# Depthwise convolutions of the gate on VectorE instead of TensorE, with dP copies moved to ScalarE and half of the X sums to GpSimd

## The chip, the cores and the metric

The kernel runs on one core of one Trainium2 chip. The metric is the device time of one execution in microseconds (us). TensorE is written PE, VectorE DVE, ScalarE ACT, GpSimd POOL and SyncE SP, as in the profile; PEld is the weight loading of PE.

## The reference

Forward and backward pass of a speech block with an attention branch and a gated convolution branch, for x of 2 x 4000 x 144 (batch, tokens T, channels D) in bfloat16. The outputs are the block's output and the gradients of x and of seven weights. Cut to what matters here:

```python
def _fwd_reference(x, w_qkv, w_att_out, w_mlp_in, dw_csgu, w_mlp_out, dw_merge, w_merge):
    xa = _layernorm(x)
    q, k, v = split(xa @ w_qkv)
    p = softmax(q @ k^T * D ** -0.5)             # 4000 x 4000 for each batch
    glob = (p @ v) @ w_att_out
    u, g = split(gelu(_layernorm(x) @ w_mlp_in))
    g = _layernorm(g)
    gc[t] = sum over i in 0..4 of g[t + i - 2] * dw_csgu[i]     # depthwise, 5 taps
    loc = (u * gc) @ w_mlp_out
    m = concat(glob, loc);  mc = depthwise 5 taps of m with dw_merge
    return x + (m + mc) @ w_merge
_out, _vjp = jax.vjp(_fwd_reference, ...);  _grads = _vjp(grad_out)
```

The backward pass of the gate needs the same five-tap convolution a second time, with the taps reversed, from the gradient of `gc` to the gradient of the normalized `g`.

## The kernel before

A sequence of 4000 tokens is laid out as 125 partitions x 32 blocks: partition p holds the tokens 32p to 32p+31, so a block is one token of each partition. Shifting by a token is shifting by a block, except at the ends of a partition, where two blocks of halo are fetched from the neighbouring partition by a DMA.

`phase_att` does one batch. Its loop runs over t = 0 to 32, one block of query rows for each t, and a step of it holds:

- four *quads* (`quad`, tags q0 to q3): scores S of block t against 1000 keys, and dP of block t-1 against another 1000, into two PSUM tiles `ps` (a pool of two). PE writes each quad with four matmuls of 500 columns over 128 channels (L1130) and four over the remaining 16 (L1136).
- `S_min` (L1154): DVE negates S from PSUM into `Pbuf` in bfloat16 with a running minimum; `P_exp` (L1162) takes the exponential on ACT.
- `PdP`: dP times P into `Sbuf`. For three of the four quads ACT copies dP out of PSUM (L1175) and DVE multiplies in SBUF (L1177); for the fourth (`direct`, q == 3) DVE multiplies straight from PSUM (L1172).
- SP transposes P and P*dP by DMA (`PT`, `ST`), and PE forms Y (L1186) and Z (L1225) from them, 32 matmuls each.
- six *X groups* (`X_group`, tags x0 to x5; five of three blocks, the last of one): PE sums the gradient's contributions for key blocks (L1270), and DVE adds the PSUM result to the accumulator `acc` (L1276).
- a share of the *local units* of the gate branch (`local_units`). These go in 16 rounds for each batch, two blocks at a time: `z_unit`, `e_tanh`, `e_h`, `e_stats`, `dug_unit`, `e_gn`, `e_dgc`, `e_m`, `e_gp` for a new pair, and for an older pair `gc_unit`, `e_du`, `dgn_unit`, `e_dh`, `dhT_unit`, and every second round the weight gradients `dwc_unit` and `dwi_unit`.

The convolutions run on PE. `t_unit` transposes a pair's normalized gate and its gradient (L534), and a stack of five blocks of the 16 channels above 128 (L539); ACT copies the result to `gT` and `gS` (L540, L542). `gc_unit` (12 matmuls, L551 and L553) multiplies by diagonal matrices of the taps, and ACT copies its result to `gc` (L554). `dgn_unit` (12 matmuls, L566 and L568) does the gradient's convolution the same way, with one column more that yields its sum over the channels; DVE reads it from PSUM (L572, L576, L584). Small PSUM results, X groups among them, share the pool `ps_w`. The diagonal matrices are built in the head, by POOL (`conv` in `Head`, L291 to L305).

The order of each engine's instructions in the loop is not the program's. `Planner.plan` runs a list scheduler over all instructions of t = 2 to 30 (batch 0) and t = 0 to 30 (batch 1), with a cost for each instruction (`cost`) and a lead for each class of instruction (the table `LEAD`, added to its position in the program), and pins the order that it finds on PE, DVE, ACT, POOL and SP. The instructions of one engine then run strictly in that order.

Of the kernel before, what the change touches and what calls it, by code (L numbers as in the profile page):

```python
# [14 lines left out]
D = 144  # L15
DR = 16
# [92 lines left out]
class Head:  # L109
# [159 lines left out]
    def conv(self):  # L269
# [18 lines left out]
        colS = wt.tile([80, 2], BF, name="colS")  # L288
        with nc.allow_non_contiguous_dma(reason="tiny conv weight column"):
            for kk in range(5):  # L290
                nc.gpsimd.dma_start(colS[kk * DR:(kk + 1) * DR, 0:1], k.dw_csgu[kk:kk + 1, 128:D].rearrange("k c -> c k"))  # L291
                nc.gpsimd.dma_start(colS[(4 - kk) * DR:(5 - kk) * DR, 1:2], k.dw_csgu[kk:kk + 1, 128:D].rearrange("k c -> c k"))
        colS32 = wt.tile([80, 2], F32, name="colS32")
        nc.gpsimd.tensor_copy(colS32[:], colS[:])
        W.dgf = wp.tile([128, 5, 128], BF, name="dgf")
        W.dgm = wp.tile([128, 5, 144], BF, name="dgm")
        for kk in range(5):
            nc.gpsimd.tensor_scalar(W.dgm[:, kk, 1:129], ident[:], cols[:, 4, kk:kk + 1], 1.0, op0=ALU.mult, op1=ALU.mult)
        nc.gpsimd.tensor_copy(W.dgf[:], W.dgm[:, :, 1:129])
        nc.gpsimd.tensor_copy(W.dgm[:, :, 0:1], cols[:, 4, :].rearrange("p (a b) -> p a b", b=1))  # L300
        W.dgs = wp.tile([80, 2, 160], BF, name="dgs")
        nc.gpsimd.memset(W.dgs[:], 0.0)
        for s in range(2):
            nc.gpsimd.tensor_scalar(W.dgs[:, s, 128 + s:D + s], W.mask[:], colS32[:, s:s + 1], 1.0, op0=ALU.mult, op1=ALU.mult)
        nc.gpsimd.tensor_copy(W.dgs[:, 1, 0:1], colS32[:, 1:2])  # L305
# [114 lines left out]
XW = 160  # L420


def local_units(k, W, b, S, A, es, DHT, ps_w):
# [7 lines left out]
    gdr = [pl.tile([PB, 2, G2, D], BF, name="gd%d" % i) for i in range(NR + 3)]  # L431
    rem = pl.tile([PB, 2, NB + 4, DR], BF, name="gd_rem")

    def gd(c):
        return gdr[{0: NR, NG2: NR + 1, NG2 + 1: NR + 2}.get(c, c % NR)]
# [3 lines left out]
    gT = [pl.tile([128, 4, PB], BF, name="gT%d" % i) for i in range(4)]  # L439
    gS = [pl.tile([80, 4, PB], BF, name="gS%d" % i) for i in range(2)]  # L440
# [12 lines left out]
    gc = pl.tile([PB, G2, D], BF, name="l_gc")  # L453
    dd = pl.tile([PB, G2, 2 * D], BF, name="l_dd")
# [55 lines left out]
    def e_dgc(g):  # L510
        t = gd(g + 1)
        nc.vector.tensor_tensor(t[:, 1], dugr[slot(g)][:], hg[:, :, 0:D], op=ALU.mult)
        nc.gpsimd.tensor_copy(rem[:, :, G2 + G2 * g:2 * G2 + G2 * g, :], t[:, :, :, 128:D])
        if g == NG2 - 1:
            nc.sync.dma_start(gd(0)[1:PB], t[0:PB - 1])
            nc.gpsimd.tensor_copy(rem[:, :, 0:G2, :], gd(0)[:, :, :, 128:D])
        if g == 0:
            nc.sync.dma_start(gd(NG2 + 1)[0:PB - 1], t[1:PB])
            nc.gpsimd.tensor_copy(rem[:, :, NB + 2:NB + 4, :], gd(NG2 + 1)[:, :, :, 128:D])
# [9 lines left out]
    def t_unit(c, g):  # L529
        pt = ps_w.tile([128, 8, 128], BF, tag="w")  # L530
        t = gd(c)
        for a in range(2):
            for bi in range(G2):
                nc.tensor.transpose(pt[:, 2 * a + bi, 0:PB], t[:, a, bi, 0:128], W.ident[0:PB, 0:PB])  # L534
        if g is not None:
            for a in range(2):
                for bi in range(G2):
                    j = G2 * g + bi
                    nc.tensor.transpose(pt[0:80, 4 + 2 * a + bi, 0:PB], rem[:, a, j:j + 5, :].rearrange("p a b -> p (a b)"), W.ident[0:PB, 0:PB])  # L539
        nc.scalar.copy(gT[c % 4][:], pt[:, 0:4, 0:PB])  # L540
        if g is not None:
            nc.scalar.copy(gS[g % 2][:], pt[0:80, 4:8, 0:PB])  # L542

    def col(a, h):
        return gT[(h // G2) % 4][:, 2 * a + h % G2, :]

    def gc_unit(g):
        pc = ps_w.tile([PB, G2, D], F32, tag="w")
        for bi in range(G2):
            i = G2 * g + bi  # L550
            nc.tensor.matmul(pc[:, bi, :], gS[g % 2][:, bi, :], W.dgs[:, 0, 0:D], start=True, stop=False)  # L551
            for kk in range(5):
                nc.tensor.matmul(pc[:, bi, 0:128], col(0, i + kk), W.dgf[:, kk, :], start=False, stop=(kk == 4))  # L553
        nc.scalar.copy(gc[:], pc[:])  # L554
        ug = ugr[g % 2]
        nc.vector.tensor_tensor(ug[:], ur[slot(g)][:], gc[:], op=ALU.mult)
        nc.sync.dma_start(S.ug_d[:, G2 * g:G2 * g + G2, :], ug[:])
# [4 lines left out]
    def dgn_unit(g):  # L562
        pd = ps_w.tile([PB, G2, D + 1], F32, tag="w")
        for bi in range(G2):
            i = G2 * g + bi
            nc.tensor.matmul(pd[:, bi, :], gS[g % 2][:, 2 + bi, :], W.dgs[:, 1, 0:D + 1], start=True, stop=False)  # L566
            for kk in range(5):
                nc.tensor.matmul(pd[:, bi, 0:129], col(1, i + 4 - kk), W.dgm[:, kk, 0:129], start=False, stop=(kk == 4))  # L568
        rs, t = rsr[slot(g)], gd(g + 1)
        s2 = sm.tile([PB, G2], F32, tag="s2")  # L570
        for bi in range(G2):
            nc.vector.scalar_tensor_tensor(gc[:, bi, :], pd[:, bi, 1:D + 1], -1.0 / D, t[:, 0, bi, :], op0=ALU.mult, op1=ALU.mult, accum_out=s2[:, bi:bi + 1])  # L572
# [3 lines left out]
        nc.vector.scalar_tensor_tensor(c0[:], pd[:, :, 0], -1.0 / D, rs[:, 0:G2], op0=ALU.mult, op1=ALU.mult)  # L576
        for bi in range(G2):
            nc.gpsimd.tensor_scalar(w_[:, bi, :], t[:, 0, bi, :], nc1[:, bi:bi + 1], c0[:, bi:bi + 1], op0=ALU.mult, op1=ALU.add)
        live["pd"] = pd

    def e_dh(g):
        pd, rs = live["pd"], rsr[slot(g)]
        for bi in range(G2):
            nc.vector.scalar_tensor_tensor(dd[:, bi, D:2 * D], pd[:, bi, 1:D + 1], rs[:, bi:bi + 1], w_[:, bi, :], op0=ALU.mult, op1=ALU.add)  # L584
        nc.vector.tensor_tensor(dhr[g % 2][0:PB, :, 0:2 * D], dd[:], gpr[slot(g)][:], op=ALU.mult)
# [18 lines left out]
    def dwc_unit(g, part):  # L604
        pw = ps_w.tile([128, 512], F32, tag="w")
        bl = blocks(g)
        for n_, (gg, bi) in enumerate(bl):
# [6 lines left out]
            else:  # L614
                nc.tensor.matmul(pw[:, 0:128], gnb(i + 4), t[:, 1, bi, 0:128], start=first, stop=last, skip_group_check=True)
                nc.tensor.matmul(pw[0:80, 128:128 + D], rem[:, 0, i:i + 5, :].rearrange("p a b -> p (a b)"), t[:, 1, bi, :], start=False, stop=last, skip_group_check=True)
# [23 lines left out]
    def round_(n, o, c):  # L640
# [6 lines left out]
        tr = [(t_unit, c, c - 2 if c is not None and c >= 2 else None)]  # L647
# [4 lines left out]
        if c is None:  # L652
            tr = [None]
        for u_ in (new[0:3] + old[0:1] + new[3:5] + old[1:2] + new[5:7] + old[2:3] + new[7:9] + old[3:4] + new[9:10] + tr + end):
            if u_ is not None:
                add(*u_)
    round_(NG2 - 1, None, None)
    round_(0, None, 0)
    round_(1, None, 1)
    add(t_unit, 2, 0)  # L660
    for r in range(1, NG2 - 1):
        round_(r + 1 if r + 1 < NG2 - 1 else None, r - 1, r + 2)
    round_(None, NG2 - 2, NG2 + 1)
    round_(None, NG2 - 1, None)
# [5 lines left out]
dgn_un D.c:-370 D.l_gc:1726 D.nc:1278 P:-1400 P.l_w:2039  # L670
dhT_un S.dhT:-339
dug_un A.dugr:-1281 P:769
dwc_un0 A.l_fl:-1231 P:-2308 P.A_dwc:-176
dwc_un1 A.l_fl:-4398 P:-1151 P.A_dwc:-3945
dwi_un A.l_fl:-1330 P:204 P.A_dWiT:-1509
e_dgc D.gd:-543 P.gd_rem:-1405 S.gd:363
e_dh D.dhr:961 D.l_dd:235
e_du D.l_dd:2463
e_gn D.rsr:-997 P.gd:92
e_gp D.gpr:587 D.l_sq:1333  # L680
e_h D.l_hg:3382 P.l_q:2377
e_m D.l_z:1356 P.l_th:178
e_stat D.mv:-666 D.st:929 D.ve:1242 P.rsr:-5337 P.ur:-1767
e_tanh A.l_th:245 D.l_z:3163 P.l_a:-417
ex0 A.Pbuf:-3070
ex1 A.Pbuf:151
ex2 A.Pbuf:-598
ex3 A.Pbuf:1201
gc_uni A.l_gc:-3041 D.ugr:1422 P:-4451 S.ug_d:-2908
jm A.qz:2610 P:1843 P.qz:2359  # L690
jt S.qt:-2111
pd0 A.Sbuf:-3029 D.Sbuf:678
pd1 A.Sbuf:-34 D.Sbuf:-1662
pd2 D.Sbuf:1485
pd3 A.Sbuf:-3176 D.Sbuf:1319
pt S.PT:-1721
q0 P:800
q1 P:-1073
q2 P:-555
q3 P:-1767  # L700
sm0 D.Pbuf:-873
sm1 D.Pbuf:-191
sm2 D.Pbuf:-3971
sm3 D.Pbuf:-1539 D.nm:860
st0 S.ST:-357
st1 S.ST:-548
t_unit A.gS:1141 A.gT:-4603 P:-694
x0 D.acc:-903 P:-2106
x1 D.acc:-793 P:-110
x2 D.acc:-2067 P:1051  # L710
x3 D.acc:1510 P:725
x4 D.acc:-1103 P:-719
x5 D.acc:1346 P:2323
y0 P:1135
y1 A.ty:-43 A.yn:-422 D.dj:-4076 D.nd:-2446 D.rl:-1315 P:-1860 P.QBs:-1255 P.g:-2227 S.Yn_d:-1439
z0 P:1770
z1 D.qz:-99 P:756 S.Zn_d:-1843
z_unit0 A.l_hs:2644 A.l_sq:-515 P:-810
z_unit1 A.l_hs:1237 A.l_sq:1980 P:-1529 P.l_a:413
zt S.zt:1300  # L720
# [5 lines left out]
class Planner:  # L726
# [55 lines left out]
    def cost(self, e, ins):  # L782
# [14 lines left out]
        if e == "DVE":  # L797
# [10 lines left out]
            return d, d + 0.085  # L808
        if e == "Activation":
            d = (0.125 if n < 200 else 0.0) + (0.06 if psum else 0.05) + n * (0.00096 if kind == "InstActivation" and (n > 300 or not psum) else 0.00081)  # L810
# [4 lines left out]
        return d, d + 0.06  # L815
# [1250 lines left out]
```

## Time and profile before

| | |
|---|---|
| median of 3 runs | 1343.8 us (1340.99 to 1346.27) |
| the profiled execution | 1346.5 us, its span 1344.5 us, granted PE clock 0.966 |
| busy, us | PE 1269.1, PEld 1043.6, DVE 1055.5, ACT 762.5, POOL 545.8 |
| planned loops | from about 76 to 579 us and from about 705 to 1229 us of the span |
| DMA | 186.6 MB, mean 139 GB/s |

The remaining time is the head (weights, layer norm, the first two steps), the end of each batch (weight gradients, output) and the end of the kernel. Busy times of an engine are those in which at least one of its instructions runs; the time of a group of instructions in the profile is the sum over them, and neighbours can overlap by some tens of nanoseconds. The step from the start of one instruction to the start of the next one that follows at once is called its pitch here.

### The profile page before, as it was taken

What the parts mean: (1) busy time and instruction counts of PE and PEld (TensorE: products, weight loads), DVE (VectorE), ACT (ScalarE), POOL (GpSimd) and SP (SyncE); (2) the same over time, 40 slices, a digit from 0 to 9 for tenths busy, and PEclk for the clock granted to TensorE, in tenths of its full rate; (3) what the DMA queues carried; (4) which work ended last, traced back from release to release, by engine and by line L of the source; (5) the groups of instructions that cost most, each with busy time, mean ns of one, the idle gap of its engine ahead of it and who ended that gap; (6) DMA issues with size and microseconds to landing.
All of it is one profiled execution on the core that took longest, in us unless ns stands there. A gap on an engine that the chain in (4) does not pass through costs nothing.

```text
span 1344.5 us, 38722 instructions
## 1 busy us (share of the span) xinstructions
PE 1269.1 (94%) x15698; PEld 1043.6 (78%) x15698; DVE 1055.5 (79%) x2816; ACT 762.5 (57%) x1232; POOL 545.8 (41%) x1083
## 2 busy tenths in 40 slices
PE   5889999999999999978788999999999999999898
PEld 3557788788888777868785788788888887888897
DVE  7368989898888888856736897988888888887574
ACT  4656665666566665533625666566666566555381
POOL 7264344434334343237613443443434334334330
PEclk9799999999999999998897999999999999999899
DMA  4278998998989989965224999998988999988412
GB/s 120 53 135 135 165 149 147 160 156 148 157 150 150 153 143 160 144 142 160 66 66 83 168 161 154 154 151 144 160 160 144 163 155 156 158 164 172 131 43 72
DMA packets 629153, 186.64 MB, mean 139 GB/s; under 512 B 611951, under 2 KB 623873, under 8 KB 628932
## 3 DMA queue, kind: packets, MB, share of 16 engines
q1 hardware_dynamic: 623338, 171.84, 72.3%
q0 software_dynamic: 5088, 12.11, 3.4%
q8 instruction: 123, 2.02, 0.6%
q14 instruction: 56, 0.46, 0.1%
q10 hardware_dynamic: 548, 0.21, 0.1%
HBM read 21.04 MB, written 14.12 MB: 26 GB/s over the span
## 4 chain that ended last, share of the span: by engine, by line
PE 74%; DVE 10%; DMA 7%; ACT 3%; POOL 3%; issue 2%; SPq 0%; DVEq 0%; POOLq 0%; ACTq 0%
PE X L1270 18%; PE ps L1130 14%; PE yz L1225 9%; PE yz L1186 8%; PE ps L1136 6%; DMA ST<-Sbuf 3%; PE po L1619 3%; DVE Pbuf L1154 2%; PE pc L553 1%; DMA go_h<-in_grad_out_dram 1%; PE pj L1093 1%; PE pd L568 1%; DVE t L1645 1%; PE pd L501 1%; DVE acc L1276 1%
## 5 line engine op out<-in xcount | busy, mean ns | idle before, releaser
L1154 DVE TENSOR_SCALAR_CACHE_REDUCE Pbuf<-ps 125x1000 bf16<-125x1000 f32 x256 | 306.3, 1196 | 88.8 <-PE ps L1136 86.9
L1162 ACT ACTIVATE Pbuf<-Pbuf,nm 125x1000 bf16<-125x1000 bf16 x256 | 278.4, 1128 | 107.9 <-DVE nm L1156 107.5
L1270 PE MATMUL X<-QBs,Sbuf 125*125 125x144 bf16 x2048 | 301.9, 231 | 0.3 <-DVE acc L1276 0.3
L1270 PE MATMUL X<-QBs,Pbuf 125*125 125x144 bf16 x2048 | 296.7, 228 | 2.3 <-POOL QBs L1208 2.3
L1270 PEld LDWEIGHTS <-Sbuf 125*125 125x125 bf16 x2048 | 263.9, 139 | 29.2 <-issue 28.9
L1130 PE MATMUL ps<-xaT_m,qt 128*125 128x500 bf16 x1024 | 269.7, 383 | 8.8 <-DVE Pbuf L1154 2.9
L1175 ACT CAST Sbuf<-ps 125x1000 bf16<-125x1000 f32 x189 | 188.1, 995 | 142.9 <-PE ps L1136 141.9
L1270 PEld LDWEIGHTS <-Pbuf 125*125 125x125 bf16 x2048 | 265.1, 139 | 1.1 <-issue 1.0
L1276 DVE TENSOR_TENSOR acc<-X,acc 125x432 f32<-125x432 f32 x372 | 200.5, 550 | 48.4 <-PE X L1270 47.2
L1130 PEld LDWEIGHTS <-qt 128*125 128x125 bf16 x1024 | 124.7, 139 | 52.5 <-issue 9.6
L1225 PE MATMUL yz<-xa_aug,ST 125*125 125x144 bf16 x2048 | 155.0, 231 | 10.5 <-DMA ST<-Sbuf 8.3
L1225 PEld LDWEIGHTS <-ST 125*125 125x125 bf16 x2048 | 141.6, 140 | 21.6 <-DMA ST<-Sbuf 11.8
L1177 DVE TENSOR_TENSOR Sbuf<-Sbuf,Pbuf 125x1024 bf16<-125x1024 bf16 x189 | 135.1, 715 | 12.3 <-ACT Sbuf L1175 10.1
L1186 PE MATMUL yz<-xa_aug,PT 125*125 125x145 bf16 x2048 | 142.8, 228 | 1.1 <-DMA PT<-Pbuf 1.1
L1186 PEld LDWEIGHTS <-PT 125*125 125x125 bf16 x2048 | 136.1, 138 | 2.7 <-issue 1.3
L1136 PEld LDWEIGHTS <-qt 16*125 16x125 bf16 x1024 | 37.3, 129 | 103.7 <-issue 103.7
L1136 PE MATMUL ps<-XR,qt 16*125 16x500 bf16 x1016 | 114.2, 426 | 0.0
L1172 DVE TENSOR_TENSOR Sbuf<-ps,Pbuf 125x1000 bf16<-125x1000 f32 x67 | 79.9, 1192 | 3.7 <-PE ps L1136 2.3
L1105 POOL COPY qz<-qz 125x48 bf16<-125x48 bf16 x124 | 31.6, 284 | 109.0 <-ACT qz L1095 108.7
L1204 POOL TENSOR_SCALAR QBs<-qz,rl 125x144 bf16<-125x144 bf16 x64 | 25.1, 392 | 119.9 <-DVE rl L1192 90.2
L596 POOL TENSOR_TENSOR A_dwc<-l_fl,A_dwc 128x512 f32<-128x512 f32 (+2 forms) x48 | 37.5, 780 | 82.7 <-ACT l_fl L595 82.6
L1619 PE MATMUL po<-VUl,YT 128*125 128x144 bf16 x640 | 54.2, 232 | 7.1 <-ACT goT L352 7.1
(549 smaller groups left out, 2346.2 us busy)
## 6 DMA issues: line engine op xcount, KB each, us to landing
Yn_d<-yn SPq DMA_DIRECT2D x64, 35.2 KB
Zn_d<-qz SPq DMA_DIRECT2D x64, 35.2 KB
ug_d<-ugr SPq DMA_DIRECT2D x32, 70.3 KB
xo<-in_x_dram SPq DMA_DIRECT2D x16, 140.6 KB
out_dram<-dxo SPq DMA_DIRECT2D x16, 140.6 KB
go_h<-in_grad_out_dram POOLq DMA_DIRECT2D x4, 504.0 KB, 6.7
Zn<-Zn_d SPq DMA_DIRECT2D x4, 504.0 KB
ST<-Sbuf SPq DMA_TRANSPOSE x124
```

What stands on the lines that cost most here:

```text
L1130: mm = nc.tensor.matmul(pp[r // 2][:, r % 2, 0:CH], QT[i][:, 3 * h, 0:PB], xaTm[:, c * CH:(c + 1) * CH], start=True, stop=False)
L1136: nc.tensor.matmul(pp[r // 2][:, r % 2, 0:CH], QT[i][rs, 1 + h, 0:PB], xr, start=False, stop=True)
L1154: nc.vector.tensor_scalar(pv(Pbuf, i % NPB, c2), src, -1.0, 3.0e38, op0=ALU.mult, op1=ALU.min, accum_out=NM[i][:, c2:c2 + 1])
L1162: nc.scalar.activation(v, v, ACT.Exp, bias=NM[i][:, 4:5], scale=-1.0)
L1172: nc.vector.tensor_tensor(pv(Sbuf, i % NDB, c2), src, pv(Pbuf, i % NPB, c2), op=ALU.mult)
L1175: nc.scalar.copy(pv(Sbuf, i % NDB, c2), src)
L1177: nc.vector.tensor_tensor(sc, sc, pchunk(i % NPB, c2), op=ALU.mult)
L1186: nc.tensor.matmul(Y, PT[0:PB, j, 0:PB], xaa[:, j, 0:D + 1], start=(j == 0), stop=(j == NB - 1))
L1225: nc.tensor.matmul(Z, ST[0:PB, j, 0:PB], xaa[:, j, 0:D], start=(j == 0), stop=(j == NB - 1))
L1270: nc.tensor.matmul(X[:, jj, :], l, r, start=(n_ == 0), stop=(n_ == len(ops) - 1))
L1276: nc.vector.tensor_tensor(av, X[:, 0:nj, :], av, op=ALU.add)
L1619: nc.tensor.matmul(po[:, q, :], YT[h][:, (i + kk) * PB:(i + kk + 1) * PB], VU[h][:, kk, :], start=(n_ == 0), stop=False)
```

## The change

- `t_unit` is gone, with `gT`, `gS` and the diagonal matrices. The taps are kept as `W.cw`, one copy for each partition, loaded by one broadcast DMA, with a second, reversed set that POOL copies.
- `conv` on DVE: products of shifted blocks with the taps in bfloat16, SBUF to SBUF, then three additions. All blocks of the gate lie in one tile `gd`; a ring of five pairs plus three fixed ones breaks the run of shifts into pieces, one to seven products for each convolution. `gc_unit` and `dgn_unit` call it.
- the sum of the gradient over the channels (before, the extra PE column) is taken by ACT with an accumulating copy (`l_aj`).
- dP is copied by ACT in all four quads inside the loop (`DIRECT` is empty).
- X groups 0, 2 and 4 (`XP`), in the planned part of the loop: ACT copies PSUM to `xs` (two buffers, float32) and POOL adds to `acc`.
- `LEAD` has new values (before, from -5337 to 3382; now from -14396 to 11658), and some costs in `cost` are changed.

In numbers of instructions, over both batches: 272 transposes and 768 matmuls leave PE, with 68 PSUM copies of `t_unit` and 32 of `gc` on ACT. DVE gets 172 products (72 of 144 elements, 40 of 288, 28 of 864, 32 of 1440) and 192 additions (64 of 576, 128 of 288); 61 products from PSUM become products in SBUF; 162 additions to `acc` of 432 elements leave it. ACT gets 61 dP copies, 162 copies of X and 64 sums. POOL gets the 162 additions.

```diff
-        W.dgf, W.dgm, W.dgs = ...  (diagonal matrices; 10 small DMAs for their weights)
+        W.cw = wp.tile([PB, 2, 5, D], BF, name="cw")
+        nc.gpsimd.dma_start(W.cw[:, 0]..., k.dw_csgu...partition_broadcast(PB))
         for kk in range(5):
+            nc.gpsimd.tensor_copy(W.cw[:, 1, kk, :], W.cw[:, 0, 4 - kk, :])
...
-    def t_unit(c, g):
...
+    def conv(a, g, dst):
+        kk = 0
+        while kk < 5:
+            h = G2 * g + kk
+            q = pos(h)
+            n = 0
+            while kk + n < 5 and pos(h + n) == q + n and pos(h + n + 1) == q + n + 1:
+                n += 1
+            for bi in ((None,) if n else (0, 1)):
+                if bi is None:
+                    v = gdr[:, a, q:q + n + 1, :]
+                    v = bass.AP(v.tensor, v.offset, [list(v.ap[0]), [D, n], [D, G2], [1, D]])
+                    nc.vector.tensor_tensor(pr[:, kk:kk + n], v, W.cw[:, a, kk:kk + n, :]...to_broadcast([PB, n, G2, D]), op=ALU.mult)
+                else:
+                    nc.vector.tensor_tensor(pr[:, kk, bi, :], gdr[:, a, pos(h + bi), :], W.cw[:, a, kk, :], op=ALU.mult)
+            kk += max(n, 1)
+        nc.vector.tensor_tensor(pr[:, 0:2], pr[:, 0:2], pr[:, 2:4], op=ALU.add)
+        nc.vector.tensor_tensor(pr[:, 0], pr[:, 0], pr[:, 1], op=ALU.add)
+        nc.vector.tensor_tensor(dst[:], pr[:, 0], pr[:, 4], op=ALU.add)

     def gc_unit(g):
-        pc = ps_w.tile(...); 12 matmuls; nc.scalar.copy(gc[:], pc[:])
+        conv(0, g, gc)
...
     def dgn_unit(g):
-        pd = ps_w.tile(...); 12 matmuls
+        conv(1, g, dg)
+        s1 = sm.tile([PB, G2], F32, tag="s1")
         for bi in range(G2):
+            nc.scalar.activation(aj[:], dg[:, bi, :], ACT.Copy, accum_out=s1[:, bi:bi + 1])
...
-                    PdP(t - 1, q ^ 1, ps[1], q == 3)
+                    PdP(t - 1, q ^ 1, ps[1], q in DIRECT)
...
+            elif blocks[0] // 6 in XP and u0 <= here["t"] < NB - 1:
+                xs = XS[0].tile([PB, 3, D], F32, tag="xs")
+                nc.scalar.copy(xs[:, 0:nj, :], X[:, 0:nj, :])
+                nc.gpsimd.tensor_tensor(av, xs[:, 0:nj, :], av, op=ALU.add)
             else:
                 nc.vector.tensor_tensor(av, X[:, 0:nj, :], av, op=ALU.add)
...
     def cost(self, e, ins):                                     # in Planner
-                return (5.0, 7.2) if n > 3000 else (2.5, 4.7) if n > 1000 else (1.35, 3.5)
-            return 0.5, 2.6
+                return (5.0, 8.0) if n > 3000 else (2.5, 5.0) if n > 1000 else (1.35, 3.8)
+            return 0.5, 2.9
...      (DVE costs x 1.01, POOL costs x 1.08; LEAD: all values new, no t_unit)
```

More of the change, by code (lines that the diff above doesn't have):

```diff
@@ L287, in conv @@
         nc.gpsimd.tensor_copy(W.mask[:], mask[:])
[L288 to L296, printed above, removed]
-        for kk in range(5):
[L298 to L305, printed above, removed]
+        W.cw = wp.tile([PB, 2, 5, D], BF, name="cw")
+        nc.gpsimd.dma_start(W.cw[:, 0].rearrange("p a b -> p (a b)"), k.dw_csgu.rearrange("a b -> (a b)").partition_broadcast(PB))
+        for kk in range(5):
+            nc.gpsimd.tensor_copy(W.cw[:, 1, kk, :], W.cw[:, 0, 4 - kk, :])
 def pre_tiles(k, b, S, xp, gp, sp):
@@ L527, in e_gp @@
         nc.vector.tensor_tensor(gpr[slot(g)][:], sq[:], q_[:], op=ALU.add)
-    def t_unit(c, g):
[L530 to L545, printed above, removed]
-    def gc_unit(g):
[L548 to L554, printed above, removed]
+    def conv(a, g, dst):
[10 more added lines that the diff above has]
+                    v = bass.AP(v.tensor, v.offset, [list(v.ap[0]), [D, n], [D, G2], [1, D]])
+                    nc.vector.tensor_tensor(pr[:, kk:kk + n], v, W.cw[:, a, kk:kk + n, :].rearrange("p k (b c) -> p k b c", b=1).to_broadcast([PB, n, G2, D]), op=ALU.mult)
+                else:
[4 more added lines that the diff above has]
+        nc.vector.tensor_tensor(dst[:], pr[:, 0], pr[:, 4], op=ALU.add)
+    def gc_unit(g):
+        conv(0, g, gc)
         ug = ugr[g % 2]
@@ L669 @@
 for _s in """
[L670 to L720, printed above, removed]
+dgn_un A.l_aj:-9020 D.c:4514 D.l_dg:-8077 D.l_gc:-493 D.l_pr:4473 D.nc:-10425 P.l_w:2029
+dhT_un S.dhT:-5232
@@ new lines @@
+dug_un A.dugr:979 P:2303
+dwc_un0 A.l_fl:2707 P:4800 P.A_dwc:-8348
+dwc_un1 A.l_fl:1522 P:-9162 P.A_dwc:2716
+dwi_un A.l_fl:8835 P:4107 P.A_dWiT:2046
+e_dgc D.gd:9261 P.gd_rem:192 S.gd:-13539
+e_dh D.dhr:2072 D.l_dd:3062
+e_du D.l_dd:4519
+e_gn D.rsr:-2927 P.gd:1973
+e_gp D.gpr:-10909 D.l_sq:3468
+e_h D.l_hg:361 P.l_q:5526
+e_m D.l_z:3524 P.l_th:1298
+e_stat D.mv:2259 D.st:1631 D.ve:-7977 P.rsr:-8052 P.ur:1338
+e_tanh A.l_th:-7422 D.l_z:2131 P.l_a:-14387
+ex0 A.Pbuf:2168
+ex1 A.Pbuf:-8252
+ex2 A.Pbuf:2807
@@ new lines @@
+ex3 A.Pbuf:-12902
+gc_uni D.l_gc:956 D.l_pr:11525 D.ugr:-7743 S.ug_d:2992
+jm A.qz:2963 P:11658 P.qz:-9741
+jt S.qt:-11083
+pd0 A.Sbuf:2717 D.Sbuf:-8749
+pd1 A.Sbuf:2811 D.Sbuf:-5099
+pd2 A.Sbuf:-11023 D.Sbuf:4116
+pd3 A.Sbuf:1681 D.Sbuf:-10091
+pt S.PT:-9751
+q0 P:-8377
+q1 P:-7795
+q2 P:-9608
+q3 P:-11238
+sm0 D.Pbuf:2558
+sm1 D.Pbuf:-10026
+sm2 D.Pbuf:-11222
+sm3 D.Pbuf:691 D.nm:-3451
+st0 S.ST:2336
+st1 S.ST:-9031
+x0 A.xs:794 D.acc:1678 P:-2950 P.acc:1227
+x1 D.acc:2271 P:4337
+x2 A.xs:9336 D.acc:2664 P:312 P.acc:7079
@@ L721 @@
+x3 D.acc:-9052 P:-8733
+x4 A.xs:1416 D.acc:1015 P:-10032 P.acc:2999
+x5 D.acc:-7984 P:8924
+y0 P:-8943
+y1 A.ty:-7461 A.yn:-9100 D.dj:-8964 D.nd:-8355 D.rl:-13745 P:-14396 P.QBs:-8361 P.g:-12110 S.Yn_d:-14370
+z0 P:5775
+z1 D.qz:2632 P:1926 S.Zn_d:4106
+z_unit0 A.l_hs:1500 A.l_sq:1403 P:1904
+z_unit1 A.l_hs:5674 A.l_sq:5474 P:1786 P.l_a:-7883
+zt S.zt:2236
 """.strip().split("\n"):
@@ L1082, in phase_att @@
             pads()
+            XS.append(es_loc.enter_context(tc.tile_pool(name="xs%d" % b, bufs=2, side="right", reuse_waits="tile")))
             units += local_units(k, W, b, S, A, es_loc, DHT, ps_w)
```

91 lines of the change are left out of this document (54 added, 37 removed).

## The prediction

> **What bounds the kernel now.** I read the page first: busy time by engine, the slices, then the chain that ended last (PE 74% of it), then the busy time by stages of the two planned loops, the groups by form, and the timeline of single steps.
>
> ```profile
> PE 1269.1 (94%) x15698; PEld 1043.6 (78%) x15698; DVE 1055.5 (79%) x2816; ACT 762.5 (57%) x1232; POOL 545.8 (41%) x1083
> PE   5889999999999999978788999999999999999898
> DVE  7368989898888888856736897988888888887574
> ```
>
> PE is full from the fourth slice on, except where a batch ends; DVE stands at eight to nine tenths. The stages (columns: window, its length, busy us of PE, PEld, DVE, ACT and POOL with instructions, granted PE clock, DMA share, GB/s):
>
> ```profile
> 151.00:550.00 399.00, 395.92 (x4987) 323.92 (x4984) 344.95 (x872) 245.04 (x383) 155.15 (x306) 1.00 0.90 152
> 751.00:1200.00 449.00, 446.28 (x5594) 363.93 (x5592) 388.23 (x977) 277.29 (x427) 176.88 (x359) 1.00 0.91 155
> ```
>
> In these 848 us PE is busy 842.2 us (99.3%), DVE 733.2 (86%), ACT 62%, POOL 39%, at full clock. A busy PE need not be a PE that streams without gaps, so the timeline decides (start, length, engine, line, operation):
>
> ```profile
> 401.33 0.23 PE L551 MATMUL pc<-dgs,gS 80*125 80x144 bf16 x1
> 401.40 0.45 PE L553 MATMUL pc<-dgf,gT 128*125 128x128 bf16 x5
> 401.69 0.23 PE L551 MATMUL pc<-dgs,gS 80*125 80x144 bf16 x1
> 401.75 0.45 PE L553 MATMUL pc<-dgf,gT 128*125 128x128 bf16 x5
> 402.04 1.01 PE L1130 MATMUL ps<-xaT_m,qt 128*125 128x500 bf16 x4
> ...
> 402.73 0.31 DVE L556 TENSOR_TENSOR ugr<-ur,l_gc 125x288 bf16<-125x288 bf16 x1
> ...
> 402.82 0.75 POOL L476 TENSOR_SCALAR l_a<-l_sq 125x576 bf16<-125x576 bf16 x1 [0.58 <-DVE l_z L474]
> 402.95 0.77 DVE L560 TENSOR_TENSOR l_dd<-dugr,l_gc 125x288 bf16<-125x288 bf16 x1
> ```
>
> One `gc_unit` takes PE from 401.33 to 402.04: 12 matmuls in 0.71 us, 0.06 us each, with the next quad right behind. So PE's stream sets the step of about 16.6 us in the loops, and work taken out of it shortens the step until another engine is full.
>
> By the Trainium skill (Trainium Kernel Development and Optimization, Best Practices) PE is to be judged by the share of its weight loads and not by matmul busy time; here that share is 81%, and by that rule PE would have a fifth to spare and its relief would bring nothing. The pitches above speak against it (rival C).
>
> **PE.** From the first start of each unit to the start behind it, the trace gives 36 `t_unit` 15.9 us, 32 `gc_unit` 22.8, 32 `dgn_unit` 23.1: together 61.8 us, all inside the loops (76 to 579, 705 to 1229 us: 1027 us). All of it lies on the path. PE's floor for the loops: 1027 - 62 = 965 us.
>
> **DVE.** What counts for a full engine is pitch: X add to L1177 behind it 0.52 us (400.51 to 401.03), L1177 to the next 0.60, L556 to L560 above 0.22, the direct product 1.11 (405.86 to 406.97). 0.60 at 1024 elements and 0.22 at 288 give 0.52 ns an element for bfloat16 from SBUF, hence estimates of 0.145 us at 144, 0.37 at 576, 0.52 at 864, 0.81 at 1440.
>
> ```profile
> L1154 DVE TENSOR_SCALAR_CACHE_REDUCE Pbuf<-ps 125x1000 bf16<-125x1000 f32 x256 | 306.3, 1196 | 88.8 <-PE ps L1136 86.9 <-PE X L1270 1.3
> L1276 DVE TENSOR_TENSOR acc<-X,acc 125x432 f32<-125x432 f32 x310 | 182.9, 600 | 41.8 <-PE X L1270 40.9
> L1177 DVE TENSOR_TENSOR Sbuf<-Sbuf,Pbuf 125x1024 bf16<-125x1024 bf16 x189 | 135.1, 715 | 12.3 <-ACT Sbuf L1175 10.1 <-ACT Pbuf L1162 1.9
> L596 POOL TENSOR_TENSOR A_dWiT<-l_fl,A_dWiT 96x432 f32<-96x432 f32 x16 | 18.0, 1126 | 17.1 <-ACT l_fl L595 17.0
> ```
>
> - Products: 72 x 0.145 + 40 x 0.22 + 28 x 0.52 + 32 x 0.81 = 60 us; additions: 64 x 0.37 + 128 x 0.22 = 52 us. +112.
> - X groups 0, 2, 4: -162 x 0.52 = -84. Direct products: -61 x (1.11 - 0.60) = -31.
> - `dgn_unit`'s DVE operations keep their number and shape and are taken as equal.
>
> The sum is -3: DVE does as much as before (878 us of the loops by the windows, 875 after) in a shorter loop, before what follows.
>
> **DVE against POOL.** In the fence above, L560 starts while POOL's L476 runs (to 403.57) and ends at 403.72, 0.77 us instead of 0.30. This is regular: of the 288-element products of L556, 23 that start with POOL idle take 0.30 us in the mean, 9 that start during a POOL operation 0.53; a DVE operation ends 0.15 us or more after POOL's. X adds, which read PSUM, take 0.60 us either way (153 and 76 of them). DVE operations with two SBUF inputs wait for POOL, those that read PSUM do not.
>
> The Trainium skill says the same (GPSIMD Engine Reference, Key points: the SBUF interfaces are shared, contention with DVE instructions with two SBUF inputs), and it speaks against this change, which adds such instructions on both sides; the trace agrees, with the numbers above.
>
> Price: before, the large DVE operations of this kind in the loops (189 of L1177, 9 x 32 local ones: 477) lost 13.5 us to it. After, there are 250 + 288 + 172 + 192 + 128 (L572 and L584 now read SBUF) = 1030. POOL grows by 162 x 1.10 us (L596 above, 1.10 where nothing disturbs it) = 178 us, from 409 to 587 us of the loops, its share by half. Lower bound: 13.5 x 1030 / 477 x 1.45 = 42, so 28 more. Upper bound: each of the 162 long additions also catches one DVE operation for half its length, 0.5 us (four hits by the L596 forms lost 0.12 to 1.06 us): +81, 109 in all. I take 70, the middle. DVE in the loops: 875 + 70 = 945 us (903 to 984).
>
> **ACT and POOL.** ACT: +61 x 0.995 (L1175) + 162 x 0.51 (L595, 432 wide) + 64 x 0.37 (144 wide, L1199's row) - 20.8 - 18.4 - 12.9 (L540, L542, L554) = +115, from 619 to 734 us of the loops; POOL to 587. Both have a quarter or more of a 965 us loop free, so I cost them at nothing. New waits: an ACT copy to `xs` waits for PE and, two additions later, for POOL; behind it stand exponentials and dP copies, and PE waits for those to get its `ps` tile back. The cover is POOL's 40% of slack; where it is gone, each late addition costs up to 1.1 us. DVE's wait for the ACT sum stands three or more DVE instructions behind it in the new order: nothing.
>
> **Head and DMA.** Before the first local unit POOL loses ten small DMA issues (5.0 us) and the diagonals (4.4 us) and gets one DMA, which the first scaled Q (L1204) now stands behind, and five copies. This lies beside PE's 8 us wait for the first ST transpose on the chain: 0, within -5 and +3. SP keeps its transposes and writes.
>
> **Sum.** With PE's floor at 965 and DVE at 945 in the loops, both can't be full at once: each quad waits for DVE's S_min and DVE for the quad. No row shows the loss; in the 100 us in which DVE stood highest (200 to 300 us, 90.5%) PE lost nothing, which bounds it from below at 0; above stands DVE kept at that 90.5%, 945 / 0.905 = 1044, 79 more than the floor. I take 25, a third, since PE at present loses 0.7%. Against the profiled execution: 1346.5 - 62 + 25 = 1309.5. The median is 2.7 us below that execution: **1307 us**.
>
> **The rivals.**
> A, ends slower: DVE becomes the bound. Its work and the waits for POOL come to 945 us, and in order, between PSUM readers and POOL's additions, it can be filled no further than the 90.5% above: loops of 1044 us, +17, so 1361. It decides from 92% (945 / 1027) down: below that fill the kernel is slower. With the upper price of the waits, 984 / 0.95 = 1036, +9. For it: every engine gets fuller, both `ps` tiles need DVE and ACT. Against: 86.9 of DVE's 88.8 us of idle time before S_min (L1154) is waiting for PE, so DVE has not yet shown its limit.
> B: the tap products don't run at 0.52 ns an element, because of their repeated taps (a stride of zero), but at the 1.05 of X adds' pitch above 0.07 us (0.52 us for 432). 92160 elements x 0.52 ns = 48 us; DVE 993, and 25 for the loss: loops 1018, 1335. No row has such a pattern.
> C: PE's stream isn't the bound, as the weight-load share has it: the loops stay at 1027, 1344. Against: pitches, no gaps over 848 us.
> D: DMA sets the step. Its share is 0.90 and 0.91 over the loops and reaches 0.99 in steps of 17 us (943.3 to 960.6). If that is full, the loops stay at 1027: 1344. Against: the step from 910 to 925 us ran in 15.0 us with a share of 0.93.
> E: the order, pinned from a cost without the waits for POOL, slips: one late S_min of 0.5 us in each of the 61 steps beyond the loss counted: 1307 + 30 = 1337 with the sum, and beyond 1361 together with A's fill.
>
> **How the numbers follow.** Forecast 0.48, A 0.28, B 0.06, C 0.04, D 0.06, E 0.08 (half of it slower, half faster). A measurement of this kernel can tell about 0.5% (7 us) from no change. Faster: 0.48 + 0.06 + 0.04 = 0.58, of which I put 0.02 to the same because the forecast's upper end comes near: 0.56. Same: C, D and that: 0.12. Slower: 0.32. The forecast's own range: no loss at all, 1282, to 50 us, 1332. With A it reaches to 1361; below, the floor with the head's -5 is 1277. Runs of one kernel differ by 5 us (1340.99 to 1346.27), which I add at both ends: 1272 to 1366.
>
> **What would show it.** Right: PE busy by 60 us less in the loops, DVE at 93% or more in them and waiting less for ps, L556 and the additions above their free 0.30 and 0.37 us, the X additions on POOL at 1.1 to 1.4 us. Tap products of 1440 elements at about 0.9 us length refute B, 1.5 would show it. Gaps of PE behind `ps` released by DVE or ACT, with DVE's share below 92%, would show A; gaps behind ST or PT, D. The prediction is wrong if DVE's waits for POOL exceed 110 us, or if ACT waits for `xs`.

## The result, and the profile after

The changed kernel takes 1393.9 us (median of 4 runs, 1388.28 to 1396.18) against 1343.2 for the kernel before beside it: ratio 1.037 [1.033, 1.041]. It is slower by 50 us; the forecast was 1307. The profiled execution took 1395.5 us (span 1393.7, granted clock 0.97).

The page, the lines that answer to those of before:

```profile
PE 1232.8 (88%) x14658; PEld 992.5 (71%) x14658; DVE 1158.8 (83%) x3018; ACT 867.5 (62%) x1483; POOL 767.2 (55%) x1229
PE   6889998999899988878788989899889999889998
DVE  7379989898988999857736998989898999897574
```

The stages, columns as before (window, length, busy PE, PEld, DVE, ACT, POOL, clock, DMA share, GB/s):

```profile
151.00:550.00 399.00, 365.19 (x4338) 290.02 (x4337) 369.05 (x910) 276.74 (x469) 247.63 (x368) 0.99 0.84 144
800.00:1200.00 400.00, 364.96 (x4338) 290.17 (x4335) 364.58 (x872) 277.72 (x461) 244.99 (x373) 1.00 0.83 146
```

PE fell from 99.3% to 91.4% of these 799 us (365.19 + 364.96), DVE rose only from 86% to 91.8%. No engine is full. The loops run from about 76 to 597 and 722 to 1278 us: some 1076 us, 49 more than before, which is the whole loss.

The waits (who waits for whom: total us, times, longest), first two of before, then those of after:

```profile
PE ps L1130 <- DVE Pbuf L1154: 2.9, 4, 1.7
PE yz L1225 <- ACT ty L1202: 2.0, 1, 2.0
```

```profile
POOL acc L1280 <- ACT xs L1279: 116.8, 68, 6.6
DVE Pbuf L1144 <- PE ps L1121: 55.4, 58, 7.6
PE ps L1115 <- DVE Pbuf L1144: 53.8, 55, 3.2
PE yz L1227 <- ACT ty L1204: 19.4, 28, 1.7
ACT xs L1279 <- POOL acc L1280: 1.2, 1, 1.2
```

PE and S_min (L1144) now wait for each other by turns, some 54 us on either side (before, PE waited 2.9 us for S_min), so neither sets the pace alone. PE also waits 19 us for ACT's copy `ty`, 2 before. One kind of DVE wait does not stand in this view, because it lies inside the instructions. The groups by form (count | busy us, mean ns | idle before):

```profile
L1280 POOL TENSOR_TENSOR acc<-xs,acc 125x432 f32<-125x432 f32 x162 | 194.4, 1204 | 118.3 <-ACT xs L1279 116.8
L1179 DVE TENSOR_TENSOR Sbuf<-Sbuf,Pbuf 125x1024 bf16<-125x1024 bf16 x250 | 200.1, 801 | 15.3 <-ACT Sbuf L1177 14.9
L1282 DVE TENSOR_TENSOR acc<-X,acc 125x432 f32<-125x432 f32 x148 | 87.7, 599 | 34.0 <-PE X L1272 33.3
L535 DVE TENSOR_TENSOR l_pr<-gd,cw 125x1440 bf16<-125x1440 bf16 x32 | 32.4, 1013 | 1.1 <-POOL gd L502 1.0
```

L1179 was 715 ns and is 801; started with POOL idle it takes 684, started during a POOL operation 934 in the mean and up to 2540. L1282, which reads PSUM, takes 599 ns and 598 (87 and 61 of them). The timeline shows it happen (start, length):

```profile
299.06 1.28 POOL L1280 TENSOR_TENSOR acc<-xs,acc 125x432 f32<-125x432 f32 x1 [1.46 <-ACT xs L1279]
299.31 1.21 DVE L540 TENSOR_TENSOR l_pr<-l_pr 125x288 bf16<-125x288 bf16 x1
...
305.87 1.29 POOL L583 TENSOR_TENSOR A_dwc<-l_fl,A_dwc 128x512 f32<-128x512 f32 x1 [5.11 <-ACT l_fl L582]
305.96 1.97 DVE L535 TENSOR_TENSOR l_pr<-gd,cw 125x1440 bf16<-125x1440 bf16 x1
307.85 1.19 DVE L1144 TENSOR_SCALAR_CACHE_REDUCE Pbuf<-ps 125x1000 bf16<-125x1000 f32 x1
307.95 1.09 POOL L1280 TENSOR_TENSOR acc<-xs,acc 125x432 f32<-125x432 f32 x1 [0.80 <-ACT xs L1279]
```

L540 needs 0.30 us by itself and shows 1.21: POOL's addition still had 1.03 us to run, and 0.91 of it was lost. L535 needs 0.90 and shows 1.97. The addition at 307.95 falls beside S_min, which reads PSUM: neither is delayed (1.19 and 1.09 us).

Summed over DVE's instructions, the time above the free length of each one's own form is 122 us (19 before): 84 us of it beside 120 of the 162 X additions on POOL, 18 beside the flush additions (L583). How the free length is taken moves these sums by a tenth. DVE's busy time rose by 103.3 us (1055.5 to 1158.8), as much as these waits rose.

### The profile page after: what moved, and what is told of

The parts are those of the page before. It is cut to its first block, busy times and chain, and to the rows that moved or that the text cites. A ratio compares the mean times of both kernels' runs of the same rounds, so it can differ in the third digit from the quotient of the medians.

```text
span 1393.7 us, 37174 instructions
## 1 busy us (share of the span) xinstructions
PE 1232.8 (88%) x14658; PEld 992.5 (71%) x14658; DVE 1158.8 (83%) x3018; ACT 867.5 (62%) x1483; POOL 767.2 (55%) x1229
## 5 line engine op out<-in xcount | busy, mean ns | idle before, releaser
L1177 ACT CAST Sbuf<-ps 125x1000 bf16<-125x1000 f32 x250 | 249.0, 996 | 203.0 <-PE ps L1121 202.1
L1144 DVE TENSOR_SCALAR_CACHE_REDUCE Pbuf<-ps 125x1000 bf16<-125x1000 f32 x256 | 305.3, 1193 | 56.3 <-PE ps L1121 55.4
L1115 PE MATMUL ps<-xaT_m,qt 128*125 128x500 bf16 x1024 | 275.2, 386 | 63.5 <-DVE Pbuf L1144 53.8
L1280 POOL TENSOR_TENSOR acc<-xs,acc 125x432 f32<-125x432 f32 x162 | 194.4, 1204 | 118.3 <-ACT xs L1279 116.8
L1179 DVE TENSOR_TENSOR Sbuf<-Sbuf,Pbuf 125x1024 bf16<-125x1024 bf16 x250 | 200.1, 801 | 15.3 <-ACT Sbuf L1177 14.9
L1115 PEld LDWEIGHTS <-qt 128*125 128x125 bf16 x1024 | 128.8, 139 | 115.3 <-issue 75.0
L1227 PE MATMUL yz<-xa_aug,ST 125*125 125x144 bf16 x2048 | 151.1, 228 | 21.9 <-ACT ty L1204 19.4
L1282 DVE TENSOR_TENSOR acc<-X,acc 125x432 f32<-125x432 f32 (+1 forms) x210 | 105.4, 510 | 46.0 <-PE X L1272 45.3
L1279 ACT COPY xs<-X 125x432 f32<-125x432 f32 x162 | 84.3, 525 | 18.6 <-PE X L1272 16.7
L535 DVE TENSOR_TENSOR l_pr<-gd,cw 125x288 bf16<-125x288 bf16 (+2 forms) x100 | 68.6, 686 | 1.4 <-POOL gd L502 1.2
L583 POOL TENSOR_TENSOR A_dwc<-l_fl,A_dwc 128x512 f32<-128x512 f32 (+2 forms) x48 | 41.6, 866 | 47.5 <-ACT l_fl L582 47.5
```

Source lines behind the costliest of these rows:

```text
L1115: mm = nc.tensor.matmul(pp[r // 2][:, r % 2, 0:CH], QT[i][:, 3 * h, 0:PB], xaTm[:, c * CH:(c + 1) * CH], start=True, stop=False)
L1144: nc.vector.tensor_scalar(v, src, -1.0, 3.0e38, op0=ALU.mult, op1=ALU.min, accum_out=NM[i][:, c2:c2 + 1])
L1177: nc.scalar.copy(pv(Sbuf, i % NDB, c2), src)
L1179: nc.vector.tensor_tensor(sc, sc, pchunk(i % NPB, c2), op=ALU.mult)
L1227: nc.tensor.matmul(Z, ST[0:PB, j, 0:PB], xaa[:, j, 0:D], start=(j == 0), stop=(j == NB - 1))
L1279: nc.scalar.copy(xs[:, 0:nj, :], X[:, 0:nj, :])
```

## The experiments

Theory 1: the loss is DVE waiting for POOL. Theory 2: the new order (`LEAD`) is the loss. Theory 3: DVE's own added work is. "Waits" below means the sum just described. Percentages are those of the 799 us from 151 to 550 and 800 to 1200. The kernel before took 1341.4 to 1343.8 us beside these runs.

**Short POOL additions.** Every X addition on POOL cut to 6 elements, the planner's cost kept, so that the order is the same on every engine. Most of each X sum is left out.

```diff
-                nc.gpsimd.tensor_tensor(av, xs[:, 0:nj, :], av, op=ALU.add)
+                nc.gpsimd.tensor_tensor(av[:, :, 0:2], xs[:, 0:nj, 0:2], av[:, :, 0:2], op=ALU.add)
...
```

> The 162 POOL additions to acc are cut from 432 to 6 elements a partition (the rest of each X sum is left out); the order of every engine is the changed kernel's. Theory 1, waits for POOL: in the changed kernel DVE loses 122 us waiting for POOL, 84 of them behind these additions, and DVE is what fills the loops (978 us of 1076, 91%). With additions of about 0.35 us the waits fall to 40-50 us, DVE to about 900 us of the loops, and at the same fill the loops take 990 us: 1305 to 1320 us. Theory 2, the order: the pinned order is the loss; since it stays, little changes, 1370 or more. Theory 3, DVE's own work for the convolutions fills it: DVE keeps all of that, at most the 84 us go, but PE and DVE go on waiting for each other: 1340 to 1370.

1320.4 us, ratio 0.985 [0.983, 0.987], at the upper end of what theory 1 gave; waits 38 us; DVE busy 1071.7, 87 less. The additions on POOL, the first stage and PE's waits:

```profile
L1280 POOL TENSOR_TENSOR acc<-xs,acc 125x6 f32<-125x6 f32 x162 | 48.2, 299 | 150.7 <-ACT xs L1279 149.3
151.00:550.00 399.00, 383.98 (x4654) 307.52 (x4650) 360.55 (x985) 295.47 (x505) 196.31 (x390) 1.00 0.92 157
PE ps L1115 <- DVE Pbuf L1144: 21.0, 32, 2.0
PE yz L1227 <- ACT ty L1204: 5.4, 7, 1.5
```

With the order, the copies and the semaphores all kept, the length of 162 POOL additions costs 74 us, and PE comes back to 96.2%. Theory 1 holds. A rival would be that DVE and PE wait for POOL's results, which come later behind long additions; but the idle time of DVE that ends with a POOL result is 24 us in the changed kernel and 22 here (24 before), that of PE 16 and 16. The rest of the change, order included, would have made a faster kernel.

**X additions on DVE, and the convolutions alone.** `XP` empty gives all X additions back to DVE; the second run also gives the fourth dP product back to it.

```diff
-XP = (0,2,4,)
+XP = ()
-DIRECT = ()
+DIRECT = (3,)
```

> All X groups added by DVE from PSUM again (XP empty), the rest as in the changed kernel, order planned with the same leads. Theory 1, waits for POOL: DVE gets 162 x 0.52 = 84 us of work and loses the 84 us of waits behind POOL's additions: DVE stays at about 978 us in the loops, time 1395 within 15 us, POOL's share back to 40%, DVE's waits for POOL at 35 to 50 us. Theory 3, DVE's own work alone: 84 us more at 91% fill, 1395 + 92 = 1485. Theory 2, the order: no number, any change of more than 20 us without a change of DVE's busy time would speak for it.

> The convolutions on DVE alone: X groups all added by DVE and the fourth dP product straight from PSUM, as before the change. Theories 1 and 3 agree: DVE in the loops 878 (before) + 112 (products and additions) + about 25 (more operations that can wait for POOL) = 1015 us; at 91% fill the loops take 1115 us, 1435 us in all (1415 to 1455). Theory 2: PE has 62 us less to do than before the change and DVE's work is no bound; 1300 to 1350.

1373.4 us (ratio 1.025 [1.021, 1.030]) and 1397.9 us (1.042 [1.039, 1.044]); both faster than theories 1 and 3 had them. Of the first, the stage:

```profile
151.00:550.00 399.00, 370.36 (x4433) 294.77 (x4430) 382.83 (x1013) 253.85 (x413) 173.81 (x306) 1.00 0.86 148
```

DVE is as long busy as in the changed kernel (1153.9 and 1158.8 us), its waits 47 us instead of 122: the 84 us of work that left it by way of POOL came back as 75 us of waits. But the same busy time as work, not waits, gives 94.7% in place of 91.8%, and 20.5 us less time. By the expectation above, more than 20 us without a change of DVE's busy time speaks for theory 2: the order has a part in the loss. The dP copy by ACT is worth 25 us here (1397.9 to 1373.4), and the two convolutions on DVE alone cost 56, all under leads that were not searched for these kernels.

**The leads of before.** The changed kernel with before's `LEAD`.

```diff
-dhT_un S.dhT:-5232
+dhT_un S.dhT:-339
-dug_un A.dugr:979 P:2303
+dug_un A.dugr:-1281 P:769
...
```

> The changed kernel with the table of leads of the kernel before (classes that it lacks have none), so another order of the same instructions. Theory 1: DVE's work and its exposure to POOL stay, 978 us within 25; time within 2% of the changed kernel, 1370 to 1420. Theory 2, the order searched anew is the loss: under 1350.

1433.5 us, ratio 1.071 [1.066, 1.076]; waits 119, DVE 88%, PE 89%. Theory 2 is out as stated: the new leads are 40 us better than the old ones. But the time also lies 13 us above theory 1's range at about the same waits, so the order counts beside them.

**Convolutions on PE.** Before, with the changed kernel's other parts: dP by ACT, X groups 0, 2 and 4 by ACT and POOL (`xs` in bfloat16, and one copy of the diagonals replaced by a view, for room), its leads and costs.

```diff
...
-                    PdP(t - 1, q ^ 1, ps[1], q == 3)
...
+                    PdP(t - 1, q ^ 1, ps[1], False)
+            elif blocks[0] // 6 in (0, 2, 4) and u0 <= here["t"] < NB - 1:
+                nc.scalar.copy(xs[:, 0:nj, :], X[:, 0:nj, :])
+                nc.gpsimd.tensor_tensor(av, xs[:, 0:nj, :], av, op=ALU.add)
...
```

> The kernel before with only the rest of the change: dP copied by ACT in all quads and X groups 0, 2, 4 through ACT and POOL (xs in bfloat16, to fit), convolutions on PE, leads and costs of the changed kernel. Theory 1, waits for POOL on a full DVE: DVE in the loops 878 - 84 - 31 + about 45 of waits (half the operations with two SBUF inputs) = 808 us, far from full; PE sets the loops at 1027 us as before: 1340 to 1360. If POOL's additions cost through their latency or through ACT, whatever DVE's load: 1370 or more.

1394.6 us, ratio 1.038 [1.034, 1.042]: a miss by 35 us. PE has gaps (95.9%) though DVE stands at 75.6% and waits only 56 us. Either the leads, searched for other instructions, or the path over POOL: settled below.

**Half the convolutions, and a planner with the lock.** The first keeps only `gc_unit`'s convolution on DVE (`dgn_unit`, with half of `t_unit`, back on PE), `XP` empty. The second is the changed kernel with a planner in which POOL and a two-input DVE operation exclude each other, leads unchanged.

```diff
     def dgn_unit(g):
-        conv(1, g, dg)
+        pd = ps_w.tile([PB, G2, D + 1], F32, tag="w")
...
-XP = (0,2,4,)
+XP = ()
```

```diff
...
+                    if e == "Pool" or (e == "DVE" and self.two(G["ins"][0])):
+                        late = max(0.0, port - s - 0.14)
+                        G["d"] += late
+                        G["end"] += late
+                        port = s + (G["end"] if e == "Pool" else G["d"])
```

> Half of the change: the forward convolution (gc_unit) on DVE, the gradient's (dgn_unit, with half of t_unit) on PE, dP copied by ACT, all X groups added by DVE. Theory 1: DVE in the loops has 998 us of e2 (X on DVE) - 56 (one convolution) - about 10 of waits = 932 us, PE 965 + 31 = 996 us; PE is the longer one again: loops at 97 to 98% of PE, 1017 us, 1336 us in all (1325 to 1345), even with or a little below the kernel before. If DVE's convolution work as such is the trouble, half of e2's loss stays: 1357.

> The changed kernel, but the planner counts POOL operations and DVE operations with two SBUF inputs as excluding each other when it makes the order; same instructions, same leads. If the loss beyond the waits themselves (DVE at 92% here, 95% with X on DVE) comes from an order made without them: 10 to 25 us faster than the changed kernel, 1370 to 1384, with DVE's waits near 120 us as before. If the waits alone count, whatever the order: 1394 within 7.

The half convolution: 1338.0 us, ratio 0.996 [0.994, 0.998], as expected, already a little below before. The planner: 1460.4 us, ratio 1.086, waits 91 us, DVE 84%, a miss by both expectations. Fewer waits and 66 us slower: it seems that leads searched with one set of costs do not fit another. So each of the runs above with changed instructions also carries an order that was not searched for it. The remaining runs take that out.

**Orders made with the waits.** Four kernels with unchanged instructions (before, the changed one, the half convolution, convolutions on PE), planned so that a two-input DVE operation ends 0.15 us after a POOL operation beside it, each with leads searched anew under that planner; then the one with all X additions on DVE.

```diff
...
+                    if e == "Pool":
+                        pool = s + G["d"]
+                    elif e == "DVE" and pool > s + 0.05 and self.two(G["ins"][0]):
+                        late = max(0.0, pool + 0.15 - (s + G["d"]))
+                        G["d"] += late
+                        G["end"] += late
```

> The kernel before with the same instructions in another order: the planner now lets a VectorE operation of two SBUF inputs end no sooner than 0.15 us after a GpSimd operation that runs beside it (the wait as the traces show it), and the leads were searched anew with that. It is the measure for the three runs beside it. TensorE's stream stays the bound; it lost 0.7% in the loops of before, VectorE's waits for GpSimd were about 19 us: 1325 to 1343 us by every theory.

> The changed kernel with the same instructions, planned with VectorE's waits for GpSimd and leads searched with them. Theory 1 (the loss is VectorE waiting for GpSimd, in an order made without knowing of it): a part of the 122 us of waits is avoided by placing reads of PSUM beside the additions; without the additions' length it was 1320 us, with them 1394: 1345 to 1375 us, VectorE's waits for GpSimd between 60 and 100 us and VectorE busy above 93%. Rival (the waits follow from the number of long GpSimd additions and of VectorE operations, whatever the order): 1385 us or more, waits near 120 us. Even by theory 1 it stays slower than before.

> Only the forward convolution on VectorE (the gradient's on TensorE), dP by ScalarE, no X addition on GpSimd, now planned with the waits and leads searched for it. It was 1338 us with leads searched for other instructions, with TensorE busy 97.2% of the loops. TensorE's floor is about 23 + 8 us (the forward convolution's matmuls and half the transposes) below that of before. Theory 1: the order gives most of that back, 1305 to 1325 us, the fastest of all. Rival (TensorE and VectorE cannot both be this full whatever the order): 1333 us or more.

> Convolutions on TensorE, dP by ScalarE, X groups 0, 2 and 4 by ScalarE and GpSimd: the kernel that took 1395 us with leads searched for other instructions, planned with the waits and leads of its own. If that loss was the order: 1330 to 1355 us, TensorE above 98.5% of the loops. If it was the path over GpSimd (TensorE's PSUM tiles held until ScalarE and GpSimd are done): 1375 us or more with TensorE still near 96%.

> Both convolutions on VectorE, dP by ScalarE, all X additions on VectorE: the kernel that took 1373 us with leads searched for other instructions, planned with VectorE's waits for GpSimd and leads of its own. The order of its own took 43 us from the kernel with the convolutions on TensorE and 23 us from the one with one convolution on VectorE, 11 us from the changed kernel. If moving the X additions to GpSimd was the changed kernel's mistake and the rest of it is sound: 1335 to 1352 us, so 30 to 50 us below the changed kernel with an order of its own (1383 us), the change without its GpSimd additions about equal to before. If the second convolution on VectorE is the mistake as well, because VectorE is then as good as full: 1360 us or more.

| kernel, own order | us | ratio to before | PE, DVE | waits, us |
|---|---|---|---|---|
| before | 1343.8 | 1.002 [1.001, 1.004] | 99.3%, 85.9% | 17 |
| changed | 1383.4 | 1.031 [1.028, 1.034] | 92.7%, 93.3% | 106 |
| half convolution | 1315.1 | 0.980 [0.977, 0.983] | 99.2%, 92.2% | 36 |
| convolutions on PE | 1351.5 | 1.007 [1.005, 1.009] | 98.7%, 77.6% | 55 |
| X additions on DVE | 1350.8 | 1.005 [1.003, 1.008] | 94.0%, 95.3% | 36 |

Before gains nothing; its PE is 99.3% full, so it could gain little from any order and does not tell what another search would have brought the others. The convolutions on PE took 43 us less: their 1395 us was the order. With PE full, the path over ACT and POOL brings nothing and costs 8 us against before's own order. The changed kernel regained 11 us, less than either theory had it (expected at most 1375, or at least 1385).

Its planner's rule was too mild. Of 40 products L1179 that start during an X addition in the changed kernel's trace, 35 lose the time that POOL still has to run (0.20 to 1.07 us) less 0.13 to 0.14 us: they do not end soon after POOL, they act as if they began 0.13 us before it ends. Of the other five, two start in the addition's last 0.1 us and lose nothing, two are held on by a second POOL operation, up to the 2.54 us above, and one starts 2 ns after the addition, runs undelayed, and the addition is the longer (1.65 us). Most POOL operations that start during L1179 show the same the other way round: they lose the time that L1179 still has to run less about 0.14 us.

**Orders made with the rule as traced.** The changed kernel, the one with X additions on DVE and the half convolution, with POOL's costs in the planner as measured, scalar operands of DVE no longer counted as an input, and leads searched again.

```diff
...
+                    if e == "Pool" or (e == "DVE" and self.two(G["ins"][0])):
+                        late = max(0.0, lock["DVE" if e == "Pool" else "Pool"] - 0.13 - s)
+                        G["d"] += late
+                        G["end"] += late
+                        lock[e] = s + G["d"] + (0.05 if e == "Pool" else 0.08)
```

> The changed kernel with the same instructions, its order made with the rule that the traces show for VectorE operations of two SBUF inputs and GpSimd operations: neither begins its work before 0.13 us from the end of the other's; GpSimd costs in the planner as measured (1.05 us for 432 elements). Theory 1a (the order made without the waits is the larger part of the loss): 1350 to 1368 us, waits of VectorE at 70 us or less. Theory 1b (the waits follow from the number of GpSimd additions; order can move no more than the 11 us that the coarser rule gave): 1375 us or more, waits at 100 us. By both it stays slower than before.

> The same, with all X additions on VectorE: 1351 us with the coarser rule. Both theories: a little better, 1335 to 1350 us, VectorE at 95% in the loops and waits at 30 us; the distance to the run beside it is what the GpSimd additions cost under an order made for them: 15 to 25 us by theory 1a, 30 or more by 1b.

> Only the forward convolution on VectorE, no GpSimd additions: 1315 us with the coarser rule, TensorE already at 99.2% of the loops, so little is left: 1305 to 1316 us. If it stays the fastest by 20 us or more against the run with both convolutions on VectorE, the second convolution costs more than the 31 us of TensorE's work that it saves, because VectorE is full.

1367.6 us (1.019 [1.016, 1.021]), 1344.9 us (1.002 [1.000, 1.005]) and 1309.8 us (0.976 [0.973, 0.978]). The first stage of each, in that order:

```profile
151.00:550.00 399.00, 373.44 (x4420) 297.41 (x4421) 381.46 (x933) 283.11 (x478) 261.83 (x372) 0.99 0.85 150
```
```profile
151.00:550.00 399.00, 378.76 (x4539) 301.96 (x4537) 387.92 (x1034) 257.90 (x417) 177.85 (x308) 0.99 0.89 154
```
```profile
151.00:550.00 399.00, 397.26 (x4935) 322.69 (x4934) 367.76 (x978) 262.20 (x402) 171.34 (x315) 1.00 0.79 159
```

In the changed kernel the waits did not shrink (122 us, 74 of them beside X additions; at most 70 were expected), yet the time fell by 26 us: DVE is now 94.4% full instead of 91.8%, and PE waits 21.5 us for S_min instead of 53.8:

```profile
PE ps L1121 <- DVE Pbuf L1150: 21.5, 30, 3.3
```

The order made with the waits does not avoid them; it puts PE's next need behind them less often. With both convolutions DVE is full (96.3%) and PE is not; with one, PE is at 99.4%.

So the changed kernel's 1394 us come apart, each step under an order of its own: 26 us the order (to 1368), 23 us the X additions on POOL with their ACT copies (to 1345), 35 us the second convolution on DVE (to 1310). The last version beats both kernels. The steps are as exact as the searches are equally good; the finer rule moved them by 5 to 16 us. The first step is theory 2's, and whether it needed the waits in the planner is not shown: no new search under the old rule was run. The second step is theory 1's, and the third theory 3's.

## Why the prediction was wrong

The steps that failed are the first two terms below.

- **DVE's waits for POOL** (70 us, with 28 and 109 as ends). Mis-sized: 103, above the middle and inside the ends; all such waits together are 122 us, above the 110 that the prediction named as a sign of being wrong. The upper end was built rightly: 84 us beside the X additions where it had 81, 19 elsewhere where it had 28. The lower end scaled the hits of a DVE that was less full; in the changed kernel a long POOL operation catches a DVE operation three times out of four (120 of 162), at 0.7 us a hit instead of the 0.5 of the upper end for every addition.
- **The loss from two engines that can't both be full** (25 us). Mis-sized, and the larger error: the loops lie 111 us above PE's floor (1076 - 965). DVE's 875 + 103 = 978 us fill them to 91%, where the forecast implied 945 / 990 = 95%. At that 95% the waits would have cost 978 / 0.955 = 1024, 34 us more; the fill cost the other 52. Half of those (26) come back with the last order of the same instructions.
- **Rival A** is what happened, by its own sign: PE's gaps stand behind `ps` released by DVE, with DVE's share at 91.8%. Its fill of 90.5% ("between PSUM readers and POOL's additions") and the measured 978 us of DVE give 978 / 0.905 = 1081, 54 more than 1027, so 1398 beside 1393.9. The prediction joined a high price of the waits (984 us) only with a fill of 95%, and so stopped the range at 1366. That the fill came out so near has luck in it: 90.5% is no limit, since the same instructions in another order fill DVE to 94.4%, and with X additions on DVE to 96.3%.
- **Rival E** (the pinned order slips) fits the second half: 26 us by the last runs, 30 in the prediction, which even names "beyond 1361 together with A's fill". It had a chance of 0.08. That the missing waits in the planner's costs are what makes the order slip is argued, not shown.
- **PE's 62 us**: right as work. The 272 transposes and 768 matmuls left (15698 to 14658), and where PE stays full the relief pays in full: half the convolutions take 31 us (22.8 + half of 15.9) from PE and the time falls by 32 (1341.8 to 1309.8). That also refutes rival C, and D: the same 187 MB go through the DMA queues, at 159 GB/s in the first stage, with a DMA share of 0.79. The sign, PE busy by 60 us less, did not come: 1269.1 to 1232.8 us, 36 less, and 55 with short additions (1213.8). For the same matmuls the changed kernel's PE thus shows 19 us more busy time than with short additions; why is not shown.
- **DVE's sum of -3**: right: the busy time rose by what the waits rose, as far as these sums can tell. **Rival B** is refuted: with POOL idle the 1440-element product takes 0.90 us (forecast 0.9; 1.5 would have shown B).
- **ACT and POOL at nothing**: right for the path over `xs`: ACT waits 1.2 us for it, and the kernel with the convolutions on PE carries the same path at 0.7% above before. Not right for ACT as a whole: PE's wait for `ty`, which no term held, rose from 2.0 to 19.4 us. It is 5.4 with short additions and as much work on ACT, but 19.2 with the X additions on DVE in another order, so its cause stays open. And the prediction booked the additions' 84 us as saved in DVE's sum and POOL's hold on DVE as a separate price; here the two came out equal.
- **Head and DMA at nothing**: right: outside the loops both kernels spend some 317 us.

## What to carry to other kernels

Moving elementwise work from VectorE to GpSimd can save VectorE nothing where most of what remains there reads two SBUF tensors: here 84 us of additions came back as 75 us of waits. Price a long GpSimd operation at up to its length less 0.13 us for the two-input VectorE operation that meets it, and search the order again with that price. And relieve the full engine only until the next one is full: half of this change was worth 32 us, the whole of it nothing (1345 us) before the GpSimd part took its share.

## What the runs showed of the hardware

- The wait holds up whole operations and is no sharing of bandwidth: in 35 of 40 cases a VectorE product with two SBUF inputs lost all the time until 0.13 us before the GpSimd addition's end, and most GpSimd operations that started during such a product lost it until about 0.14 us before the product's end. The prediction's "ends 0.15 us or more after POOL's" was that rule seen on operations of 0.3 us only. The Trainium skill says this too (SBUF — State Buffer, section "SBUF: two separate sides": the shared port pair is an exclusive lock that whichever of the two starts first keeps for its whole instruction); the trace agrees, but for these last 0.13 us of the length that it records.
- Equal busy time is not equal: with 1154 us of VectorE the kernel took 1373 us, with 1159 us, 75 us more of it spent in waits, 1394. We read this as waits falling where the order of the other engines did not allow for them; no run separates that from the order itself.
- A bfloat16 product whose second operand repeats with a stride of zero runs at the same pace as the others here: 0.60 us at 864 elements and 0.90 at 1440, so 0.52 ns for each further element.
